# Sliding-window attention with a fused two-layer FFN: ten weight blocks instead of thirteen decoded in the first attention stretch, and two element-wise steps moved between engines

## The chip, the cores and the metric

The kernel runs on one core of one Trainium2 chip. The metric is the device time of one execution in microseconds (us); lower is better. Engines are called PE (TensorE matmuls; PEld are its weight loads), DVE (VectorE), ACT (ScalarE), POOL (GpSimd) and SP (SyncE, which issues the DMAs here).

## What is computed

Four batches of eight heads, 768 positions, head size 64, all fp32. Each query sees the first 4 keys (the sinks) and the last 128 keys up to itself. The heads' outputs are concatenated to rows of 512, and each row goes through an FFN with 2048 hidden values and a clipped quadratic activation.

```python
scores = q @ k.T / sqrt(64)
keep   = (pos_k < 4) | ((pos_q - pos_k >= 0) & (pos_q - pos_k < 128))
a      = softmax(where(keep, scores, -1e9))
x      = concat_heads(a @ v)                  # 3072 x 512
h      = x @ w_in                             # 3072 x 2048
g      = where(h >= 1, h, where(h <= -1, 0, (h + 1) ** 2 / 4))
out    = g @ w_out
```

## The kernel before

**Work units.** Each half of a head's sequence (384 queries, three tiles of 128) is one *unit*; there are 64. Eight heads of one batch and one half are a *chunk* of 384 output rows; there are 8. The first 16 units (`NATIVE`, chunks 0 and 1) compute scores and values in plain fp32 from pair loads (`load2`, `values2`); from unit 16 on, `load` brings keys `k_r` and queries `r` and splits each into a high and a low part (L231 to L235: ACT makes the high part, POOL or DVE subtracts).

**One unit.** `scores` (L249) writes three score tiles to PSUM; a custom DVE instruction (L253) adds the mask and finds the row peak; ACT takes the exponential (L257); POOL adds a small constant to the row sums (L262), DVE inverts them (L263), and the three tiles are scaled by the result at L275 (ACT) or L277 (DVE). The string `NORM = "vaa"` says which engine scales which tile of units 0 to 15: DVE the first, ACT the other two. `transp` (L326, L336) transposes on PE, ACT copies the result out (L329), and `av2` or `av` (L369, L404) multiplies with the values.

**Weights.** The weights lie in memory as 64-bit words. Each of the 32 blocks (16 of w_in, 16 of w_out, 512 KB raw each) is loaded to a buffer `w` and decoded: three DVE integer operations (L157, L158, L159), an ACT cast to the high part (L160) and a DVE subtraction for the low part (L161). Raw and decoded blocks share a pool of 16 buffers (`wpool`), of which the decoded w_out blocks take more and more, so that late raw loads wait until an earlier raw block has been read by its L159.

**FFN.** For each hidden block j of 16, `stage1` runs 12 matmuls (L445) into `h_ps` (two buffers), then ACT (L452, L453), DVE (L454) and ACT (L455) make `g` and its high part `gh`, and L456 subtracts to the low part `gl`. `stage2` for block j comes two blocks later: nine matmuls (L464) with `gh` twice and `gl` once. In the first chunk's FFN (`row0 == 0`) `gl` is made on POOL, in all others on DVE.

**Order of the work.** PE's order is written by hand: `spread` interleaves two lists of steps by their weights. Stretch 1 is chunk 0's attention with the first `WFIRST` = 13 weight blocks; stretch 2 is chunk 1's attention with chunk 0's FFN and the remaining weight blocks; then each chunk's attention runs beside the FFN of the chunk before it. On the other engines a scheduler sets the order when the program is built. Until the end of stretch 2 the loads go out on SP's queue in the order of the program (`fetch`), so a load that waits for a buffer holds back all loads behind it.

```python
prev = wsteps[:WFIRST]                                           # L514, stretch 1
prev = spread(wsteps[WFIRST:], prev, WLEAD)                      # L529, joins stretch 2
eng = NORM[i] if units.index(u) < NATIVE else "v"                # L273
(nc.gpsimd if row0 == GL_POOL else nc.vector).tensor_tensor(gl, g, gh.bitcast(F32), op=ALU.subtract)
```

Of the kernel before, what the change touches and what calls it, by code (L numbers as in the profile page):

```python
# [8 lines left out]
F32 = mybir.dt.float32  # L9
# [4 lines left out]
ALU = mybir.AluOpType  # L14

B, H, S, D = 4, 8, 768, 64
# [11 lines left out]
NATIVE = 16  # L28


KL_POOL = range(16, 20)
GL_POOL = 0
NORM = "vaa"

CHECK = range(34, 34 + 2 * NJ)
WFIRST = 13
AHEAD = 3

LAG = 2
# [9 lines left out]
def attn_ffn(ctx, tc, qk, vx, vs, qp, vp, par, w_in, w_out, out):  # L51
    nc = tc.nc
# [185 lines left out]
    def scores(u, i):  # L238
        b, h, t0 = u
        qs, k_s = st["qk", u]  # L240
        if i == 0:
            st["p", u] = [att.tile([P, CT, 260], F32, name="p"), att.tile([P, 2 * CT], F32, name="stat")]
        p, stat = st["p", u]
        t = t0 + i
        lo = KB if t == 0 else 0
        c0 = i * KB if t0 else max(0, (i - 1) * KB)
        ps = ps_a.tile([P, 512], F32, name="ps_a")
        for j, q in enumerate(qs):
            nc.tensor.matmul(ps[:, lo:260], lhsT=q[:, i * P:(i + 1) * P], rhs=k_s[:, c0:c0 + 260 - lo],  # L249
                             start=(j == 0), stop=(j == len(qs) - 1))  # L250
        peak_i = peak[:, units.index(u), i:i + 1]
        m = (m0, m1n if units.index(u) < NATIVE else m1, m2)[min(t, 2)]
        found = nc.vector.tensor_tensor_reduce(  # L253
            out=p[:, i, lo:260], in0=ps[:, lo:260], in1=m, scale=-0.125, scalar=3.0e38,
            op0=ALU.add, op1=ALU.min, accum_out=peak_i)
        last_max.append(found)
        nc.scalar.activation(p[:, i, lo:260], p[:, i, lo:260], AF.Exp, bias=peak_i, scale=-1.0,  # L257
                             accum_out=stat[:, i:i + 1])
        if i < CT - 1:
            return  # L260
        st.pop(("qk", u))
        nc.gpsimd.tensor_scalar(stat[:, CT:2 * CT], stat[:, 0:CT], 1.0e-9, None, op0=ALU.add)  # L262
        nc.vector.reciprocal(stat[:, CT:2 * CT], stat[:, CT:2 * CT])  # L263
        i0 = int(t0 == 0)
        c0 = 0
        if units.index(u) >= NATIVE:

            c0 = P
            nc.vector.tensor_tensor(p[:, i0:, KB:260], p[:, i0:, KB:260], p[:, i0:, 0:P], op=ALU.add)
        for i in range(CT):  # L270
            lo = KB if t0 + i == 0 else c0
            r = stat[:, CT + i:CT + i + 1]
            eng = NORM[i] if units.index(u) < NATIVE else "v"  # L273
            if eng == "a":
                nc.scalar.activation(p[:, i, lo:260], p[:, i, lo:260], AF.Copy, scale=r)  # L275
            else:
                (nc.gpsimd if eng == "p" else nc.vector).tensor_scalar(p[:, i, lo:260], p[:, i, lo:260], r, None,  # L277
                                                                       op0=ALU.mult)
        if units.index(u) < NATIVE:
            sk = None  # L280
        else:
            sk = att.tile([P, CT * NSINK], F32, name="sk")[:, :(CT - i0) * NSINK]
            nc.vector.tensor_copy(sk.rearrange("p (i s) -> p i s", s=NSINK), p[:, i0:, P:KB])
        st["p", u] = (p, sk)
# [128 lines left out]
    units = [(b, h, t0) for b, t0 in chunks for h in range(H)]  # L413

    def attn_steps(n):
        us = {k: units[n - k] for k in (-1, 0, 1, 2) if 0 <= n - k < len(units)}
        steps = []
        for deep, late, f in ((3, 4, load2), (2, 1, values2)):
            for p in range(NATIVE // 2):
                if n == (2 * p - late if p >= deep else 0):  # L420
                    steps.append((0.0, lambda p=p, f=f: f(*divmod(p, H // 2))))
        if n == 0:
            steps = [steps[i] for i in (0, 3, 1, 4, 2)]
        if n + 1 >= NATIVE and -1 in us:
            steps.append((0.0, lambda: load(us[-1])))
        if 1 in us and n - 1 >= NATIVE:
            steps.append((0.0, lambda: values(us[1])))
        qk = [(0.43 if n < NATIVE else 0.22, lambda i=i: scores(us[0], i)) for i in range(CT) if 0 in us]
        tp = [(0.43, lambda i=i: transp(us[1], i)) for i in range(2 if n - 1 < NATIVE else 1) if 1 in us]
        pv = [(1.0, lambda: av(us[2]))] if 2 in us else []  # L430
        if 2 in us and n - 2 < NATIVE:
            pv = [(1.6, lambda: av2(units[n - 3]))] if n % 2 else []
        steps += qk + tp + pv
        if n in CHECK:
            steps.append((0.0, lambda: recheck(n - CHECK[0], min(n, len(units) - 1))))
        return steps


    def stage1(x, j, ct, hs, row0):
        T = CT * P  # L440
        if ct == 0:
            hs[j] = ps_h.tile([P, 512], F32, name="h_ps")
        h_ps = hs[j]
        for n, (w, y) in enumerate(((0, 0), (0, 1), (1, 0))):
            nc.tensor.matmul(h_ps[:, :T], lhsT=w_i[j][:, w, ct * P:(ct + 1) * P], rhs=x[:, y, ct],  # L445
                             start=(ct == 0 and n == 0), stop=(ct == NCT - 1 and n == 2))
        if ct < NCT - 1:
            return
        g = moe.tile([P, T], F32, name="g")
        gh = moe3.tile([P, T], F32R, name="gh")  # L450
        gl = moe3.tile([P, T], F32R, name="gl")
        nc.scalar.activation(g, h_ps[:, :T], AF.Relu, bias=half, scale=0.5)  # L452
        nc.scalar.activation(g, g, AF.Square)  # L453
        nc.vector.scalar_tensor_tensor(g, g, 1.0, h_ps[:, :T], op0=ALU.min, op1=ALU.max)  # L454
        nc.scalar.copy(gh, g)  # L455
        (nc.gpsimd if row0 == GL_POOL else nc.vector).tensor_tensor(gl, g, gh.bitcast(F32), op=ALU.subtract)  # L456
        hs[j] = gh, gl

    def stage2(o_ps, hs, j, tt, row0):
# [18 lines left out]
    def moe_steps(row0, tail):  # L478


        x = xpool.tile([P, 2, NCT, CT * P], F32R, name="x")
        o_ps, hs = [], {}
        steps = [(0.0, lambda ct=ct: split(x, ct)) for ct in range(NCT)]
        second = tail[:]
        for j in range(NJ):
            if j < LAG:
                steps += second[j * CT:(j + 1) * CT]
            steps += [(0.49, lambda j=j, ct=ct: stage1(x, j, ct, hs, row0)) for ct in range(NCT)]
            if j >= LAG:
                steps += [(0.65, lambda j=j - LAG, tt=tt: stage2(o_ps, hs, j, tt, row0)) for tt in range(CT)]  # L490
        tail[:] = [(0.65, lambda j=j, tt=tt: stage2(o_ps, hs, j, tt, row0)) for j in range(NJ - LAG, NJ)
                   for tt in range(CT)]
        return steps

    def spread(a, b, lead=1.0):

        wa, wb = (sum(w for w, _ in s) for s in (a, b))
        steps, n, da, db = [], 0, 0.0, 0.0
        for step in b:
            while n < len(a) and da * lead * wb <= db * wa:  # L500
                steps.append(a[n])
                da += a[n][0]
                n += 1
            steps.append(step)
            db += step[0]
        return steps + a[n:]
# [6 lines left out]
    first.append(early.enter_context(tc.tile_pool(name="first", bufs=3)))  # L513
    prev = wsteps[:WFIRST]  # L514
    n0 = 0
    tail = []
    for c in range(len(chunks)):
# [10 lines left out]
        if c == 0:  # L528
            prev = spread(wsteps[WFIRST:], prev, WLEAD)  # L529

# [143 lines left out]
```

## Time and profile before

| | |
|---|---|
| time, median of 3 runs | 725.88 us (724.31 to 726.3) |
| profiled execution: its own time, its span | 726.5 us, 724.8 us |
| PE busy, PEld busy | 97%, 85% of the span |
| DVE, ACT, POOL busy | 73%, 70%, 42% |
| mean granted PE clock | 0.992 |
| chain that ended last, by engine | PE 70%, DVE 13%, ACT 6%, DMA 5%, POOL 3% |

The span is the time from the first to the last instruction. The chain that ended last is followed back from the last instruction, at each step to what released it. "Idle before" is time in which an engine stood still, with the instruction or transfer that ended it. Stretch 1 lasts to about 54 us, where the first FFN matmul starts; stretch 2 to about 144 us.

### The profile page before, as it was taken

To read this page: it belongs to the slowest core of one execution; us is meant where nothing else is said; L and a number is where in the kernel's file an instruction comes from. 1 tells how busy PE (TensorE), PEld (TensorE's weight loads), DVE (VectorE), ACT (ScalarE), POOL (GpSimd) and SP (SyncE) were. 2 spreads that over 40 slices of the span, in tenths; PEclk is the share of its full clock that TensorE was granted. 3 is DMA by queue.
4 is the path that set the end of the run, shared out by engine and by line. 5 is a ranking of instruction groups with operands and counts; after the bars stand their busy time and mean duration, and the time that the engine had idled before them with its cause. 6 is when DMAs were issued, how large, how long until landed. Compare 5 with 4: busy or idle time off the path is not lost.

```text
span 724.8 us, 12264 instructions
## 1 busy us (share of the span) xinstructions
PE 699.7 (97%) x3841; PEld 615.6 (85%) x3841; DVE 529.4 (73%) x1393; ACT 504.4 (70%) x1313; POOL 305.7 (42%) x529
## 2 busy tenths in 40 slices
PE   6879999999999999999999999999999999999996
PEld 4547778899989999999889998999989989989895
DVE  8988989578786777687887887878877787833221
ACT  5887677687776777687677877778777867644432
POOL 3002224755453545455564666645556365500000
PEclk9989999999999999999999999999999999999999
DMA  7453453222221322153242533334323342101001
GB/s 291 146 225 127 188 193 121 58 89 58 57 57 33 96 65 66 46 186 114 88 125 64 170 126 115 115 103 137 122 82 127 107 125 74 67 1 44 0 1 48
DMA packets 38568, 73.54 MB, mean 101 GB/s; under 512 B 6752, under 2 KB 21088, under 8 KB 38496
## 3 DMA queue, kind: packets, MB, share of 16 engines
q1 hardware_dynamic: 38496, 72.68, 31.2%
q8 instruction: 32, 0.52, 0.3%
q14 instruction: 40, 0.33, 0.1%
HBM read 66.37 MB, written 6.29 MB: 100 GB/s over the span
## 4 chain that ended last, share of the span: by engine, by line
PE 70%; DVE 13%; ACT 6%; DMA 5%; POOL 3%; issue 2%; POOLq 0%; ACTq 0%; SPq 0%; DVEq 0%
PE h_ps L445 28%; PE o_ps L464 28%; PE ps_a L249 6%; PE ps_a L404 4%; ACT p L257 2%; PE ps_a L336 2%; DVE k_s L233 2%; DMA k_r<-qk 1%; DVE p L277 1%; PE ps_a L369 1%; PE ps_a L326 1%; DMA r<-vx 1%; DVE gl L456 1%; ACT k_s L231 1%; DMA r<-qk 1%
## 5 line engine op out<-in xcount | busy, mean ns | idle before, releaser
L445 PE MATMUL h_ps<-x,wi 128*128 128x384 f32 x1536 | 310.1, 340 | 0.0
L445 PEld LDWEIGHTS h_ps<-x,wi 128*128 128x128 f32 x1536 | 262.7, 188 | 10.8 <-issue 2.7
L464 PE MATMUL o_ps<-w,gh 128*128 128x512 f32 x768 | 243.6, 398 | 0.0
L464 PE MATMUL o_ps<-w,gl 128*128 128x512 f32 x384 | 150.9, 393 | 0.3 <-POOL gl L456 0.3
L464 PEld LDWEIGHTS o_ps<-w,gh 128*128 128x128 f32 x768 | 134.1, 188 | 15.8 <-issue 1.4
L454 DVE SCALAR_TENSOR_TENSOR g<-g,h_ps 128x384 f32<-128x384 f32 x128 | 70.2, 548 | 66.4 <-ACT g L453 65.5
L452 ACT ACTIVATE g<-h_ps,half 128x384 f32<-128x384 f32 x128 | 73.9, 577 | 62.0 <-PE h_ps L445 61.6
L257 ACT ACTIVATE p<-p,peak 128x260 f32<-128x260 f32 (+1 forms) x192 | 94.0, 490 | 30.7 <-DVE peak L253 29.2
L235 POOL TENSOR_TENSOR q_l<-r,q_h 128x384 fp32r<-128x384 f32 x48 | 50.4, 1049 | 131.9 <-ACT q_h L234 121.6
L455 ACT CAST gh<-g 128x384 fp32r<-128x384 f32 x128 | 65.5, 511 | 53.0 <-DVE g L454 52.1
L456 DVE TENSOR_TENSOR gl<-g,gh 128x384 fp32r<-128x384 f32 x112 | 70.2, 627 | 24.7 <-ACT gh L455 23.7
L464 PEld LDWEIGHTS o_ps<-w,gl 128*128 128x128 f32 x384 | 72.0, 188 | 18.2 <-POOL gl L456 0.8
L253 DVE CUSTOM_DVE_ANT_0 p<-ps_a,m 128x260 f32<-128x260 f32 (+1 forms) x176 | 68.2, 398 | 16.6 <-PE ps_a L249 15.9
L233 DVE TENSOR_TENSOR k_s<-k_r,k_s 64x524 fp32r<-64x524 f32 (+1 forms) x44 | 47.2, 1073 | 42.8 <-ACT k_s L231 42.7
L453 ACT ACTIVATE g<-g 128x384 f32<-128x384 f32 x128 | 67.0, 524 | 2.6
L348 POOL TENSOR_SCALAR_AFFINE_SELECT pt<-pt 128x384 fp32r<-128x384 f32 (+1 forms) x96 | 50.3, 525 | 23.8 <-DVE pt L341 21.8
L277 DVE TENSOR_SCALAR p<-p,stat 128x132 f32<-128x132 f32 (+1 forms) x160 | 56.8, 404 | 0.2
L262 POOL TENSOR_SCALAR stat<-stat 128x3 f32<-128x3 f32 x64 | 28.6, 447 | 66.1 <-ACT p L257 61.4
L346 POOL TENSOR_SCALAR_AFFINE_SELECT pt<-pt 128x384 fp32r<-128x384 f32 (+1 forms) x96 | 52.6, 549 | 6.9 <-ACT pt L340 2.7
L404 PEld LDWEIGHTS ps_a<-pt,v_s 128*128 128x128 f32 x304 | 46.5, 188 | 2.2
L404 PE MATMUL ps_a<-pt,v_s 128*128 128x256 f32 (+1 forms) x304 | 46.4, 272 | 0.0
L249 PE MATMUL ps_a<-k_s,q_h 128*128 128x260 f32 (+1 forms) x144 | 40.4, 281 | 4.4 <-DVE sk L343 3.1
(116 smaller groups left out, 986.1 us busy)
## 6 DMA issues: line engine op xcount, KB each, us to landing
r<-qk SPq DMA_DIRECT2D x48, 192.0 KB
k_r<-qk SPq DMA_DIRECT2D x32, 262.0 KB
w<-w_in SPq DMA_DIRECT2D x16, 512.0 KB
w<-w_out SPq DMA_DIRECT2D x16, 512.0 KB
again<-w_in SPq DMA_DIRECT2D x16, 512.0 KB
again<-w_out SPq DMA_DIRECT2D x16, 512.0 KB
out<-o SPq DMA_DIRECT2D x23, 256.0 KB
r<-vx SPq DMA_DIRECT2D x32, 128.0 KB
```

The costliest lines, as they stand in the source:

```text
L249: nc.tensor.matmul(ps[:, lo:260], lhsT=q[:, i * P:(i + 1) * P], rhs=k_s[:, c0:c0 + 260 - lo], start=(j == 0), stop=(j == len(qs) - 1))
L253: found = nc.vector.tensor_tensor_reduce(out=p[:, i, lo:260], in0=ps[:, lo:260], in1=m, scale=-0.125, scalar=3.0e38, op0=ALU.add, op1=ALU. ...
L257: nc.scalar.activation(p[:, i, lo:260], p[:, i, lo:260], AF.Exp, bias=peak_i, scale=-1.0, accum_out=stat[:, i:i + 1])
L277: (nc.gpsimd if eng == "p" else nc.vector).tensor_scalar(p[:, i, lo:260], p[:, i, lo:260], r, None, op0=ALU.mult)
L404: nc.tensor.matmul(z, lhsT=w, rhs=y, start=(n == 0), stop=(n == len(mms) - 1))
L445: nc.tensor.matmul(h_ps[:, :T], lhsT=w_i[j][:, w, ct * P:(ct + 1) * P], rhs=x[:, y, ct], start=(ct == 0 and n == 0), stop=(ct == NCT - 1 a ...
L452: nc.scalar.activation(g, h_ps[:, :T], AF.Relu, bias=half, scale=0.5)
L453: nc.scalar.activation(g, g, AF.Square)
L454: nc.vector.scalar_tensor_tensor(g, g, 1.0, h_ps[:, :T], op0=ALU.min, op1=ALU.max)
L455: nc.scalar.copy(gh, g)
L456: (nc.gpsimd if row0 == GL_POOL else nc.vector).tensor_tensor(gl, g, gh.bitcast(F32), op=ALU.subtract)
L464: nc.tensor.matmul(o_ps[tt], lhsT=gg[:, tt * P:(tt + 1) * P], rhs=w_o[j][:, w], start=(j == 0 and n == 0), stop=(j == NJ - 1 and n == 2))
```

## The change

`WFIRST` falls from 13 to 10: three weight blocks move from stretch 1 to stretch 2. `gl` of the first chunk is made on DVE as in all other chunks. `NORM` gets an entry for each of the first two chunks: units 8 to 15 scale their first tile on ACT instead of DVE.

```diff
-GL_POOL = 0
-NORM = "vaa"
+NORM = ("vaa", "aaa")
 ...
-WFIRST = 13
+WFIRST = 10
 ...
-            eng = NORM[i] if units.index(u) < NATIVE else "v"
+            eng = NORM[units.index(u) // H][i] if units.index(u) < NATIVE else "v"
 ...
-        (nc.gpsimd if row0 == GL_POOL else nc.vector).tensor_tensor(gl, g, gh.bitcast(F32), op=ALU.subtract)
+        nc.vector.tensor_tensor(gl, g, gh.bitcast(F32), op=ALU.subtract)
```

The changed file is one line shorter, so that in its rows below every line number is one less (L158 there is L159 before).

The first place is DVE in stretch 1, units 8 and 9, from the inversion of unit 8's sums to the next unit's first peak. Before:

```order
L263 RECIPROCAL stat<-stat 128x3
L253 ISA p,peak<-ps_a,m_106 128x260
L253 ISA peak 128x1
L157 TENSOR_SCALAR o<-w 128x512
L277 TENSOR_SCALAR p<-p,stat 128x128
L161 TENSOR_TENSOR w<-o,w 128x512
L158 SCALAR_TENSOR_TENSOR o<-w,o 128x512
L263 RECIPROCAL stat<-stat 128x3
L159 SCALAR_TENSOR_TENSOR o<-w,o 128x512
L277 TENSOR_SCALAR p<-p,stat 128x128
L161 TENSOR_TENSOR wi_157<-o,wi_157 128x512
L253 ISA p,peak<-ps_a,m_109 128x128
```

The same stretch of a pair in the changed kernel (units 4 and 5):

```order
L262 RECIPROCAL stat<-stat 128x3
L252 ISA p,peak<-ps_a,m_106 128x260
L252 ISA peak 128x1
L156 TENSOR_SCALAR o<-w 128x512
L276 TENSOR_SCALAR p<-p,stat 128x128
L160 TENSOR_TENSOR wi_154<-o,wi_154 128x512
L157 SCALAR_TENSOR_TENSOR o<-w,o 128x512
L262 RECIPROCAL stat<-stat 128x3
L158 SCALAR_TENSOR_TENSOR o<-w,o 128x512
L276 TENSOR_SCALAR p<-p,stat 128x128
L252 ISA p,peak<-ps_a,m_109 128x128
```

One subtraction fewer stands between the pair's last scaling and the next peak; the rows ahead of that are the same kinds in the same order.

The second place is DVE late in stretch 2, around the decode of the block `wi14` (raw load `w_1155` before, `w_1198` now). `p_1367` before and `p_1363` now are unit 16's scores, `g_1326` is the activation of hidden block 10. Before:

```order
L161 TENSOR_TENSOR w_1249<-o_1250,w_1249 128x512
L159 SCALAR_TENSOR_TENSOR o_1297<-w_1155,o_1297 128x512
L157 TENSOR_SCALAR o_1337<-w_1247 128x512
L158 SCALAR_TENSOR_TENSOR o_1337<-w_1247,o_1337 128x512
L161 TENSOR_TENSOR wi14_165<-o_1297,wi14_165 128x512
L159 SCALAR_TENSOR_TENSOR o_1337<-w_1247,o_1337 128x512
L454 SCALAR_TENSOR_TENSOR g_1326<-g_1326,h_ps_1303 128x384
L161 TENSOR_TENSOR w_1336<-o_1337,w_1336 128x512
L253 ISA p_1367,peak_97<-ps_a_1369,m0_109 128x128
```

With the change:

```order
L453 SCALAR_TENSOR_TENSOR g_1326<-g_1326,h_ps_1297 128x384
L157 SCALAR_TENSOR_TENSOR o_1283<-w_1159,o_1283 128x512
L157 SCALAR_TENSOR_TENSOR o_1314<-w_1198,o_1314 128x512
L252 ISA p_1363,peak_97<-ps_a_1365,m0_109 128x128
L252 ISA peak_97 128x1
L252 ISA p_1363,peak_97<-ps_a_1374,m1_107 128x260
L252 ISA peak_97 128x1
L455 TENSOR_TENSOR gl_1328<-g_1326,gh_1327 128x384
L158 SCALAR_TENSOR_TENSOR o_1283<-w_1159,o_1283 128x512
L252 ISA p_1363,peak_97<-ps_a_1388,m2_106 128x260
L252 ISA peak_97 128x1
L158 SCALAR_TENSOR_TENSOR o_1314<-w_1198,o_1314 128x512
```

The third integer operation of `wi14` (L159 before, L158 now) stood ahead of hidden block 10's `g` and of unit 16's first peak; now it stands behind both and behind unit 16's last peak.

The third place is SP's queue in the changed kernel at the same point. The second row is the load of the w_in block that gets `wi14`'s raw buffer, the third and fourth are unit 17's keys and queries:

```order
L145 DMA w<-w_out 128x1024
L145 DMA w<-w_in 128x1024
L145 DMA k_r<-qk 128x392
L145 DMA r<-qk 128x384
L145 DMA w<-w_out 128x1024
```

Before, the same rows stand in the same order: nothing moved here.

## Rows read from the trace of the kernel before

**Rows 1.** The page's first part: busy time, share of the span and instructions of each engine.

```profile
PE 699.7 (97%) x3841; PEld 615.6 (85%) x3841; DVE 529.4 (73%) x1393; ACT 504.4 (70%) x1313; POOL 305.7 (42%) x529
```

**Rows 2.** Busy time by stretch of time: length, then busy us and instructions of PE, PEld, DVE, ACT and POOL, the granted PE clock, the DMA share and GB/s. The first three are periods of a pair of units in stretch 1, the rest is stretch 2.

```profile
20.80:31.00 10.20, 7.93 (x43) 4.94 (x42) 9.90 (x31) 9.12 (x31) 1.06 (x3) 0.94 0.60 216
31.00:41.20 10.20, 7.89 (x43) 4.96 (x42) 9.90 (x33) 9.01 (x28) 0.82 (x3) 0.83 0.62 220
41.20:51.40 10.20, 7.81 (x41) 4.96 (x40) 9.28 (x30) 8.81 (x27) 0.46 (x2) 0.83 0.61 223
...
54.40:94.00 39.60, 39.60 (x209) 29.88 (x209) 34.24 (x80) 29.26 (x79) 8.62 (x11) 1.00 0.40 144
94.00:119.00 25.00, 25.00 (x132) 19.45 (x131) 23.77 (x49) 17.43 (x45) 8.31 (x8) 1.00 0.54 190
119.00:132.60 13.60, 13.31 (x84) 11.41 (x84) 13.35 (x34) 10.28 (x30) 9.72 (x12) 1.00 0.31 93
```

**Rows 3.** PE in order of time, stretch 1, units 8 and 9 (start, length, operation, count; in brackets the idle time before it and what ended it).

```profile
41.16 2.40 PE L369 MATMUL ps_a<-pt,v_s 128*64 128x128 f32 x12
...
43.75 1.36 PE L249 MATMUL ps_a<-qp 64*128 64x128 f32 x6
...
49.82 0.80 PE L326 MATMUL ps_a<-ident,p 128*128 128x128 f32 x2 [2.05 <-ACT p L275]
...
51.40 2.40 PE L369 MATMUL ps_a<-pt,v_s 128*64 128x128 f32 x12
...
54.00 0.48 PE L249 MATMUL ps_a<-qp 64*128 64x128 f32 x2
```

**Rows 4.** DVE in order of time at the end of the same pair.

```profile
53.34 0.69 DVE L161 TENSOR_TENSOR wi<-o,wi 128x512 fp32r<-128x512 f32 x1 [1.30 <-ACT wi L160]
54.52 0.29 DVE L253 CUSTOM_DVE_ANT_0 p<-ps_a,m 128x128 f32<-128x128 f32 x1 [0.49 <-PE ps_a L249]
```

**Rows 5.** DVE's groups from 10 to 55 us, by shape: count, busy us, mean ns of one, idle before.

```profile
L158 DVE SCALAR_TENSOR_TENSOR o<-w,o 128x512 int32<-128x512 int32 x13 | 8.9, 684 | 0.0
L159 DVE SCALAR_TENSOR_TENSOR o<-w,o 128x512 int32<-128x512 int32 x13 | 8.8, 677 | 0.0
L157 DVE TENSOR_SCALAR o<-w 128x512 int32<-128x512 int32 x14 | 5.9, 419 | 0.0
L161 DVE TENSOR_TENSOR wi<-o,wi 128x512 fp32r<-128x512 f32 x7 | 4.8, 687 | 2.0 <-ACT wi L160 2.0
...
L277 DVE TENSOR_SCALAR p<-p,stat 128x128 f32<-128x128 f32 x10 | 2.8, 280 | 0.1
```

**Rows 6.** The same groups of DVE from 55 to 136 us.

```profile
L158 DVE SCALAR_TENSOR_TENSOR o<-w,o 128x512 int32<-128x512 int32 x19 | 16.8, 884 | 0.2
L159 DVE SCALAR_TENSOR_TENSOR o<-w,o 128x512 int32<-128x512 int32 x19 | 15.2, 801 | 0.0
L157 DVE TENSOR_SCALAR o<-w 128x512 int32<-128x512 int32 x19 | 9.4, 493 | 2.3 <-DMA w<-w_in 2.3
...
L161 DVE TENSOR_TENSOR w<-o,w 128x512 fp32r<-128x512 f32 x10 | 7.9, 788 | 0.2 <-ACT w L160 0.2
```

**Rows 7.** POOL's largest group from 55 to 136 us.

```profile
L456 POOL TENSOR_TENSOR gl<-g,gh 128x384 fp32r<-128x384 f32 x13 | 15.3, 1178 | 31.8 <-ACT gh L455 18.5 <-issue 13.1
```

**Rows 8.** The same operation on DVE after 160 us: shortest, median and longest ns, first and last start.

```profile
L456 DVE TENSOR_TENSOR gl<-g,gh x107: 540/559/1855, 161.3 to 697.3; 128x384 fp32r<-128x384 f32 x107
```

**Rows 9.** ACT's groups from 10 to 55 us, by shape: an operation on a 128x128 tile.

```profile
L257 ACT ACTIVATE p<-p,peak 128x128 f32<-128x128 f32 x8 | 3.2, 397 | 0.9 <-POOL stat L262 0.4 <-DVE stat L263 0.3 <-DVE peak L253 0.2
```

**Rows 10.** DVE in order of time, late in stretch 2 (the first row is the L159 of `wi14`, the second hidden block 10's `g`, the third unit 16's second peak).

```profile
114.00 0.68 DVE L159 SCALAR_TENSOR_TENSOR o<-w,o 128x512 int32<-128x512 int32 x1
...
117.57 0.54 DVE L454 SCALAR_TENSOR_TENSOR g<-g,h_ps 128x384 f32<-128x384 f32 x1
...
119.55 0.42 DVE L253 CUSTOM_DVE_ANT_0 p<-ps_a,m 128x260 f32<-128x260 f32 x1
```

**Rows 11.** SP's issues in order of time at that point.

```profile
114.70 0.33 SPq L146 DMA_DIRECT2D w<-w_in  x1
115.15 0.36 SPq L146 DMA_DIRECT2D k_r<-qk  x1
```

**Rows 12.** The chain that ended last, in order of time: start, us, what.

```profile
115.15 3.68 DMA k_r<-qk
```

**Rows 13.** ACT in order of time: the high part of unit 17's keys.

```profile
118.85 0.52 ACT L231 CAST k_s<-k_r 128x392 fp32r<-128x392 f32 x1 [0.55 <-DMA k_r<-qk]
```

**Rows 14.** POOL in order of time: unit 17's keys, a `gl`, unit 17's queries.

```profile
119.50 1.03 POOL L233 TENSOR_TENSOR k_s<-k_r,k_s 64x392 fp32r<-64x392 f32 x1 [3.60 <-ACT k_s L231]
120.61 1.35 POOL L456 TENSOR_TENSOR gl<-g,gh 128x384 fp32r<-128x384 f32 x1
121.92 1.46 POOL L235 TENSOR_TENSOR q_l<-r,q_h 128x384 fp32r<-128x384 f32 x1
```

**Rows 15.** PE in order of time, stretch 2: unit 16's last score tile, unit 17's first one, and a matmul on `gl` near the end.

```profile
119.72 0.28 PE L249 MATMUL ps_a<-k_s,q_l 128*128 128x260 f32 x1
...
122.92 0.22 PE L249 MATMUL ps_a<-k_s,q_h 128*128 128x128 f32 x1
123.43 0.33 PE L249 MATMUL ps_a<-k_s,q_l 128*128 128x128 f32 x1 [0.29 <-POOL q_l L235]
...
144.75 0.50 PE L464 MATMUL o_ps<-w,gl 128*128 128x512 f32 x1 [0.33 <-POOL gl L456]
```

## The prediction

> **What bounds the kernel now.** I read the page's first part, the stretches of time, PE's timeline in stretch 1, the other engines' groups, and the timelines of all five queues around 120 us. PE is busy 97% of the span [rows 1], so only time in which PE stands still, or runs at its lower clock, can be won or lost. The stretches show two regimes [rows 2]. In stretch 1 a pair of units takes 10.2 us three times over; PE is busy under 8 us of it, and its mean granted clock falls to 0.83, which says that it spends part of each period at the lower of its two levels (1.2 and 2.4 GHz). DVE is busy 9.9 of 10.2 us there and looks like the limit. In stretch 2 PE is busy 39.6 of 39.6, 25.0 of 25.0 and 13.31 of 13.60 us at full clock: PE is the limit, and DVE runs just under it at 86%, 95% and 98%.
>
> **Is stretch 1 really bound by DVE?** The path says no. In the third period PE starts a unit's scores at 43.75, its transposes at 49.82 after 2.05 us of idling for ACT's scaled tile, the value product at 51.40, and the next scores at 54.00 [rows 3]. So 6.07 us lie between scores and transposes, and 4.18 us on PE from there to the next scores. The first part runs through DVE's peaks, three decode steps and the inversion; the second part is PE alone. At the period's end DVE waits: 1.30 us for an ACT cast and 0.49 us for PE's new scores [rows 4]. Its high share is decode work that fills slack.
>
> **The change part by part.**
>
> *Three blocks leave stretch 1.* One block costs DVE 0.42 + 0.68 + 0.68 + 0.69 = 2.47 us [rows 5], three 7.4 us (somewhat less in a full queue, since neighbours overlap). The order of the changed kernel shows which instructions go: one block per pair less, and the missing subtraction stands behind the pair's last scaling, in the second part of the period. Between a unit's peaks and its scaling the rows are of the same kinds as before. So the 6.07 us stay, and the 4.18 us are PE's own. Bounds for the stretch: a gain of 3 x 2.1 = 6.3 us if DVE's throughput were the limit after all, and nothing. I take nothing, because DVE is seen waiting at the end of the period [rows 4].
>
> *Scalings to ACT.* Eight DVE operations of 0.28 us [rows 5] become ACT operations; the nearest ACT row for that shape has 0.40 us [rows 9]. Units 10 to 15 and 9 have their transposes in stretch 2, behind PE work. Unit 8's transposes are the ones that PE waits for at 49.82, and ACT now does one more tile ahead of the two that they need: +0.4 us (bounds 0 and 0.4).
>
> *`gl` to DVE.* POOL's 13 in this window take 15.3 us [rows 7]; on DVE one takes 0.56 us [rows 8], so 13 add 7.3 us to a DVE that is 86 to 98% busy. But in this stretch the same decode steps are slower than in stretch 1: 0.88 against 0.68, 0.80 against 0.68, 0.49 against 0.42, 0.79 against 0.69 us [rows 5, 6], 0.49 us a block, 9.4 us over 19 blocks. POOL was nearly idle in stretch 1 and is mostly at `gl` here, so I give `gl` some 7 of the 9.4. The move then costs DVE about nothing (bounds: +7.3 and -2.1 us). The Trainium skill ("Perfetto Trace Analysis", section on optimizing Scalar/DVE operations) would offload a saturated DVE to ScalarE or even GpSimd, which speaks against this part; but it adds that offloading between DVE and GpSimd might not help, since they share an SBUF port. The Trainium skill's page "SBUF — State Buffer", section "Who interferes with whom", makes that an exclusive lock: a DVE instruction with two SBUF inputs and a GpSimd instruction that reads SBUF hold each other up. By the first rule alone the move costs the full 7.3 us of DVE; the slower decode steps agree with the second.
>
> PE's two short waits for POOL go: 0.29 us before unit 17's queries (counted in the next term) and 0.33 us for a `gl` at 144.75 [rows 15]: -0.3 us.
>
> *Three blocks join stretch 2.* Their 7.4 us of DVE time fit into its gaps and the quiet 10 us behind 133 us. What does not fit is the **order**. The raw load of the second last w_in block takes the buffer of `wi14`'s raw words. It goes out at 114.70, when the L159 that started at 114.00 is through [rows 10, 11]; unit 17's keys stand right behind it in SP's queue, go out at 115.15 [rows 11] and land 3.68 us later [rows 12]. ACT splits them at 118.85 [rows 13], POOL subtracts from 119.50 to 120.53, then does a `gl`, and the queries from 121.92 to 123.38 [rows 14]. PE reaches unit 17's scores at 122.92 and loses 0.29 us [rows 15]. So there are just 2.4 us of slack between the keys' end at 120.53 and 122.92.
>
> In the changed kernel that L159 stands behind hidden block 10's `g`, unit 16's three peaks and a `gl` on DVE. PE's order around units 16 and 17 hardly moves, so those keep their times. From `g` at 117.57 [rows 10] DVE has: `g` itself 0.5, two L158 1.3, three peaks 0.3 + 0.4 + 0.4, `gl` 0.56, two L159 1.3, together 4.8 us less some 0.4 of overlap: 122.0. From the other side, unit 16's last scores are written at 120.0 [rows 15], and a peak and an L159 behind them give 121.1. I take 122.0, because DVE has little idling there. From the old L159's end (114.68) to the keys' end (120.53) it is 5.85 us, and SP, DMA, ACT and POOL steps are unchanged: 127.85. The queries' subtraction, no longer behind a `gl`, takes 1.03 to 1.46 us, so the second matmul runs at about 129.0 instead of 123.43: **+5.5 us** (bounds +4.5 from 121.1, and +7 if the collisions of [rows 6] stretch DVE's steps). PE's queue is in order; the FFN matmuls behind unit 17's scores wait as well. Nothing later gives it back, because PE is the limit from there on.
>
> **Sum:** +0.4 - 0.3 + 5.5 = +5.6 us on the profiled execution's own 726.5 us, 732.1. The median of the runs shown is 0.6 us lower, so I predict **731.5 us**.
>
> **Rivals.**
> - *Stretch 1 pays for it (no change).* If DVE's throughput does set the period of a pair, it falls by up to 2.1 us three times: -6.3, with the late keys -6.3 + 5.6, 725.2 us. For it: 9.9 of 10.2 us busy [rows 2]. Against it: the waits of [rows 4].
> - *Faster.* Stretch 1 gains 3 to 6.3 us and the keys are not late, because DVE, rid of its collisions with `gl`, reaches the deciding L159 before about 117.5 us. Then 719.6 to 722.9 us. Against it: in the changed order unit 16's last peak precedes that L159, and PE writes those scores only at 120.0.
> - *Slower still.* The collisions stay (POOL's own key and query splits) and `gl` costs DVE its full 0.56 us: four more of them ahead of the L159 are +2.2 us, 733.7. It decides if the decode steps in stretch 2 stay at 0.8 to 0.9 us.
> - *The key load is not held.* If the late raw load took another buffer, only -0.3 and +0.4 remain: 726 us. Against it: the load goes out 0.02 us behind that L159's end.
>
> **How the numbers follow.** About 0.3% (2.2 us) is what a measurement of this kernel can tell from no change. Forecast and its worse form 0.66; no change (first and last rival) 0.20; faster 0.14. The forecast's own range is 729 to 735.5. The range of 724.0 to 735.5 takes in the no-change cases and leaves out the faster one and a tail above.
>
> **What would show it.** PE's timeline: an idle of 4 to 6 us before unit 17's first L249, ended by POOL or ACT on `k_s`; unit 17's key load issued at about 122.4 instead of 115.15. The first FFN matmul still at 54 to 55 us, pairs still 10.2 us. Decode steps in stretch 2 back near 0.68 us. Pairs clearly under 10 us would prove the reading of stretch 1 wrong; unit 17's keys in time would prove the main term wrong.

## The result, and the profile after

The changed kernel takes **736.43 us** (median of 4 runs, 735.75 to 737.42) against 726.09 us before: ratio 1.0141, 95% interval 1.0107 to 1.0174. The forecast was 731.5 us in a range of 724.0 to 735.5: the direction was right, the loss nearly twice as large as the sum, and the time 0.9 us above the upper end. Medians and ratios here and below leave disturbed executions out; the one profiled for e7 was such, so that e12 profiles its kernel again.

To see where the time went, each profiled execution is cut at the first matmul of hidden block 0 in the FFN of chunks 0, 1 and 2 (us; the four parts add up to the span; so cut, stretch 2 of the kernel before ends at 146.95). The last column counts the blocks that DVE had decoded at the first cut and 64.6 us later (119.0 in the kernel before).

| kernel | up to the first cut | stretch 2 | next chunk | rest | decoded |
|---|---|---|---|---|---|
| before | 54.41 | 92.54 | 81.52 | 496.31 | 13, 29 |
| before, second profile (e17) | 54.36 | 92.64 | 81.31 | 493.81 | 13, 30 |
| changed | 53.78 | 101.72 | 83.63 | 496.57 | 9, 27 |
| changed, second profile (e15) | 54.84 | 101.56 | 83.73 | 493.74 | 9, 27 |

Stretch 2 and the next chunk repeat to within 0.2 us; the first part differs by 1.1 us and the rest by 3 us between two executions of one kernel (among the kernels of the second table both spread wider). So the loss is **+9.1 us in stretch 2 and +2.3 us in the next chunk**, and nothing outside them is told apart from chance.

The first part of the page, then stretches of time as in [rows 2] (columns as there; from 119 us cut at PE's stall):

```profile
PE 703.0 (96%) x3841; PEld 616.6 (84%) x3841; DVE 526.8 (72%) x1401; ACT 506.7 (69%) x1321; POOL 287.3 (39%) x513
```

```profile
20.80:31.00 10.20, 7.97 (x45) 5.18 (x46) 8.79 (x30) 9.19 (x32) 0.84 (x3) 0.90 0.49 168
31.00:41.20 10.20, 7.89 (x46) 5.04 (x44) 7.50 (x26) 8.28 (x28) 0.45 (x2) 0.83 0.48 169
41.20:51.40 10.20, 7.40 (x42) 4.68 (x40) 7.11 (x23) 8.13 (x28) 0.61 (x2) 0.83 0.45 167
54.40:94.00 39.60, 39.49 (x209) 29.93 (x209) 35.20 (x85) 30.90 (x84) 2.66 (x4) 1.00 0.46 166
94.00:119.00 25.00, 25.00 (x132) 19.32 (x131) 22.01 (x51) 17.43 (x45) 3.45 (x4) 1.00 0.51 181
119.00:122.80 3.80, 3.33 (x21) 2.86 (x20) 3.80 (x12) 2.84 (x11) 0.00 (x0) 1.00 0.00 0
122.80:128.80 6.00, 0.46 (x2) 0.02 (x1) 5.44 (x15) 3.34 (x9) 1.76 (x2) 0.93 0.51 156
128.80:134.60 5.80, 4.96 (x16) 4.39 (x17) 4.10 (x10) 1.91 (x6) 1.19 (x1) 0.50 0.39 116
```

Two things are to be seen. In stretch 1 DVE falls from 9.9 to between 7.1 and 8.8 us of 10.2, and PE does not go faster for it. From 122.8 to 128.8 PE is busy 0.46 of 6.00 us, and in the 5.8 us behind that its granted clock is 0.50, its lower level, so that 4.96 us of work are worth half as much.

PE in order of time in stretch 1, the same pair as [rows 3]:

```profile
40.62 2.27 PE L368 MATMUL ps_a<-pt,v_s 128*64 128x128 f32 x12
...
49.37 0.88 PE L325 MATMUL ps_a<-ident,p 128*128 128x128 f32 x2 [2.23 <-DVE wi L160]
...
51.03 2.19 PE L368 MATMUL ps_a<-pt,v_s 128*64 128x128 f32 x12
```

This period is 10.4 us, against 10.2 before; in the second profile 10.7.

PE in order of time around unit 17's scores, answering to [rows 15]:

```profile
122.86 0.40 PE L463 MATMUL o_ps<-w,gl 128*128 128x512 f32 x1
128.85 0.47 PE L248 MATMUL ps_a<-k_s,q_h 128*128 128x128 f32 x1 [5.59 <-POOL k_s L232]
130.12 0.47 PE L248 MATMUL ps_a<-k_s,q_l 128*128 128x128 f32 x1 [0.79 <-POOL q_l L234]
130.39 1.16 PE L463 MATMUL o_ps<-w,gh 128*128 128x512 f32 x2
...
132.21 1.16 PE L444 MATMUL h_ps<-x,wi 128*128 128x384 f32 x3
```

And what it waits for: SP's issues, then DVE, answering to [rows 11] and [rows 10].

```profile
122.27 0.33 SPq L145 DMA_DIRECT2D w<-w_in  x1
123.09 0.33 SPq L145 DMA_DIRECT2D k_r<-qk  x1
```

```profile
117.92 0.54 DVE L453 SCALAR_TENSOR_TENSOR g<-g,h_ps 128x384 f32<-128x384 f32 x1
118.38 1.28 DVE L157 SCALAR_TENSOR_TENSOR o<-w,o 128x512 int32<-128x512 int32 x2
...
121.56 0.68 DVE L158 SCALAR_TENSOR_TENSOR o<-w,o 128x512 int32<-128x512 int32 x1
122.16 0.68 DVE L160 TENSOR_TENSOR w<-o,w 128x512 fp32r<-128x512 f32 x1
```

The third integer step of `wi14` runs at 121.56 instead of 114.00, the raw load goes out at 122.27, unit 17's keys at 123.09 instead of 115.15, and PE idles 5.59 + 0.79 us instead of 0.29.

DVE's groups from 55 to 136 us by shape, answering to [rows 6] (count, busy us, mean ns, idle before):

```profile
L157 DVE SCALAR_TENSOR_TENSOR o<-w,o 128x512 int32<-128x512 int32 x22 | 15.0, 687 | 0.1
L158 DVE SCALAR_TENSOR_TENSOR o<-w,o 128x512 int32<-128x512 int32 x21 | 14.2, 683 | 0.0
L160 DVE TENSOR_TENSOR w<-o,w 128x512 fp32r<-128x512 f32 x11 | 9.2, 834 | 0.7 <-ACT w L159 0.7
L156 DVE TENSOR_SCALAR o<-w 128x512 int32<-128x512 int32 x21 | 8.7, 423 | 3.8 <-DMA w<-w_in 3.1 <-DMA w<-w_out 0.6
L455 DVE TENSOR_TENSOR gl<-g,gh 128x384 fp32r<-128x384 f32 x12 | 8.0, 663 | 0.5 <-ACT gh L454 0.4
```

The integer steps fell from 0.88 and 0.80 to 0.69 and 0.68 us once `gl` had left POOL; the subtraction of the w_out blocks did not (0.79 to 0.83 us).

The 2.3 us of the next chunk, in PE's order and, ahead of it, ACT's:

```profile
166.91 0.59 ACT L470 COPY o<-o_ps 128x512 f32<-128x512 f32 x1 [2.64 <-DMA out<-o]
```

```profile
169.94 2.35 PE L444 MATMUL h_ps<-x,wi 128*128 128x384 f32 x12 [0.90 <-DVE g L453]
172.95 0.50 PE L463 MATMUL o_ps<-w,gl 128*128 128x512 f32 x1 [0.19 <-DVE gl L455]
...
175.73 0.36 PE L248 MATMUL ps_a<-k_s,q_h 128*128 128x260 f32 x1 [0.33 <-DVE xn L406]
```

ACT waits until the first of chunk 0's three output tiles is written, to use its buffer for the third. Exponentials and a ReLU stand behind that copy. Before, the same wait was 1.0 us and PE never felt it. PE's three waits are 1.4 us together; where the other 0.9 us went, at full clock, no row shows.

### The profile page after: what moved, and what is told of

Read it like the earlier page. It is cut to its first block, busy times and chain, and to the rows that moved or that the text cites. A ratio compares the mean times of both kernels' runs of the same rounds, so it can differ in the third digit from the quotient of the medians.

```text
span 735.7 us, 12243 instructions
## 1 busy us (share of the span) xinstructions
PE 703.0 (96%) x3841; PEld 616.6 (84%) x3841; DVE 526.8 (72%) x1401; ACT 506.7 (69%) x1321; POOL 287.3 (39%) x513
## 4 chain that ended last, share of the span: by engine, by line
PE 68%; DVE 15%; ACT 7%; DMA 4%; issue 3%; POOL 2%; ACTq 0%; SPq 0%; POOLq 0%
PE o_ps L463 27%; PE h_ps L444 27%; PE ps_a L248 6%; PE ps_a L403 3%; ACT p L256 2%; PE ps_a L368 2%; DVE gl L455 2%; DVE k_s L232 2%; PE ps_a L325 1%; PE ps_a L335 1%; DVE p L276 1%; DVE p L252 1%; DVE g L453 1%; DMA again<-w_in 1%; DMA r<-qk 1%
## 5 line engine op out<-in xcount | busy, mean ns | idle before, releaser
L455 DVE TENSOR_TENSOR gl<-g,gh 128x384 fp32r<-128x384 f32 x128 | 80.2, 627 | 27.3 <-ACT gh L454 26.3
L276 DVE TENSOR_SCALAR p<-p,stat 128x132 f32<-128x132 f32 (+1 forms) x152 | 54.9, 414 | 0.1
```

What stands on the lines that cost most here:

```text
L455: nc.vector.tensor_tensor(gl, g, gh.bitcast(F32), op=ALU.subtract)
```

## The experiments

**Theory A** (the prediction's): the loss is unit 17's key load, late because the orders of DVE and SP hold it. **Theory D**: DVE's time is what stretch 2 lacks; whatever is added to DVE there comes out as waiting of PE, at the keys or elsewhere. **Theory K**: PE's lower clock behind the idle is a loss of its own. **Theory O**: the loss in the next chunk is ACT's wait for an output buffer.

The profiled executions, cut as above:

| kernel | time, us | ratio to before | first cut | stretch 2 | next chunk | rest | decoded |
|---|---|---|---|---|---|---|---|
| e1 ten blocks only | 733.9 | 1.0105 [1.0078, 1.0132] | 54.89 | 101.12 | 81.31 | 493.70 | 9, 27 |
| e2 `gl` only | 728.47 | 1.0034 [1.0019, 1.0050] | 54.52 | 92.74 | 83.33 | 497.80 | 13, 29 |
| e3 scalings only | 726.52 | 0.9998 [0.9980, 1.0016] | 55.24 | 92.94 | 81.31 | 495.74 | 13, 29 |
| e4 keys first | 730.87 | 1.0060 [1.0040, 1.0080] | 54.13 | 98.01 | 82.08 | 494.63 | 9, 27 |
| e5 filled | 736.78 | 1.0150 [1.0129, 1.0172] | 55.48 | 99.25 | 81.77 | 498.68 | |
| e6 copy on DVE | 735.7 | 1.0133 [1.0112, 1.0153] | 54.86 | 102.17 | 83.73 | 494.92 | |
| e7, e12 keys, values | 729.6 (e12: 733.4) | 1.0062 [1.0037, 1.0086] | 55.87 | 98.74 | 82.77 | 494.21 | 10, 27 |
| e8 twelve blocks | 730.31 | 1.0059 [1.0042, 1.0077] | 56.80 | 95.49 | 82.89 | 495.02 | 11, 28 |
| e9 more DVE | 732.35 | 1.0081 [1.0066, 1.0096] | 54.51 | 98.42 | 81.35 | 497.69 | 13, 27 |
| e10 less DVE | 729.16 | 1.0036 [1.0024, 1.0049] | 54.88 | 93.85 | 84.17 | 495.63 | 9, 29 |
| e11 output buffer | 735.48 | 1.0123 [1.0103, 1.0143] | 56.65 | 102.11 | 83.01 | 495.60 | |
| e13 earlier decode | 740.08 | 1.0187 [1.0170, 1.0205] | 54.89 | 105.97 | 82.35 | 496.19 | 9, 27 |
| e14 earlier, keys | 734.88 | 1.0120 [1.0100, 1.0141] | 54.70 | 99.73 | 82.44 | 496.78 | 9, 26 |
| e16 filled, second profile | 732.3 (one run) | | 53.83 | 100.82 | 81.35 | 494.58 | |

**The three parts alone, on the kernel before.**

```diff
-WFIRST = 13
+WFIRST = 10                                   # e1
-        (nc.gpsimd if row0 == GL_POOL else nc.vector).tensor_tensor(gl, ...
+        nc.vector.tensor_tensor(gl, ...       # e2
-NORM = "vaa"
+NORM = ("vaa", "aaa")                         # e3
```

> The kernel before with WFIRST = 10 and nothing else. Theory A (order: unit 17's keys wait behind a raw load that waits for the third integer step of wi14, and it took all three decode blocks and the gl steps on DVE to push that step behind unit 16's peaks): the step stands ahead of the peaks here, so it runs between 116 and 119.5, the keys go out 2 to 5 us later than the 115.15 of before instead of 8, PE idles 0 to 3 us before unit 17's scores, and the time is 726 to 730. Rival B (the three extra blocks alone do it): idle of 5 to 6.5 us there and 734 to 737. Rival C (gl on DVE does it alone): 725 to 726.

> The kernel before with chunk 0's gl on DVE and nothing else. Theory A: the step of wi14 stands ahead of unit 16's peaks and the decode steps in stretch 2 fall back towards 0.68 us, so the keys are in time: 725 to 726, the two short waits of PE for POOL gone. Rival C (gl on DVE costs its 0.56 us each and delays the keys by itself): the keys go out 3 us late or more, 730 to 737. Rival B as A.

> The kernel before with units 8 to 15 scaling their first tile on ACT and nothing else. Theory A and rivals B and C: no place of the chain moves but unit 8's transposes, 0 to 0.4 us later: 725.5 to 726.5. A rival of its own (ACT becomes late in stretch 2): over 728.

The three blocks alone cost stretch 2 +8.6 us. That is rival B of e1 in kind, not A, though the 733.9 us lie just under B's 734 and only 3.7 of PE's 6.6 us of idle stand at unit 17's scores. In e1 the step of `wi14` stands ahead of unit 16's peaks, as A wanted, and the keys go out as late as in the changed kernel all the same; PE stalls there, and once more before that:

```profile
122.80 0.33 SPq L146 DMA_DIRECT2D k_r<-qk  x1
```

```profile
122.21 0.44 PE L326 MATMUL ps_a<-ident,p 128*128 128x128 f32 x2 [1.64 <-DVE peak L253]
...
128.41 0.33 PE L249 MATMUL ps_a<-k_s,q_h 128*128 128x128 f32 x1 [2.87 <-POOL k_s L233]
129.54 0.33 PE L249 MATMUL ps_a<-k_s,q_l 128*128 128x128 f32 x1 [0.81 <-POOL q_l L235]
```

`gl` alone costs stretch 2 nothing (+0.2 us) but brings a loss in the next chunk (+1.8 us): ACT's wait is 2.54 us there too, and 1.0 us in e1 and e3. Its 728.47 us lie between A's forecast and C's. The scalings alone cost nothing that the median can tell. The three ratios add up to the change's: 1.05, 0.34 and -0.02% make 1.37%, against 1.41%.

**Keys ahead of the late raw loads (e4).** On the changed kernel:

```diff
-            for k in range(n, min(n + min(AHEAD, NJ - n // 2 - 1) + 1, 2 * NJ)):
+            for k in range(n, min(n + (min(AHEAD, NJ - n // 2 - 1) if n != 29 else 0) + 1, 2 * NJ)):
 ...
             prev = spread(wsteps[WFIRST:], prev, WLEAD)
+            p31 = prev.index(wsteps[31]); prev.insert(p31 + 3, prev.pop(p31))
```

> The changed kernel, but the raw load of the last w_in block is issued by that block's own step, behind unit 17's keys, and the last w_out block's step three places later, behind unit 18's keys; all decode work stays. Theory A: unit 17's keys go out at 115 to 116, the idle of 6.4 us before its scores and the low clock behind it go, 8.5 us less than the changed kernel: 727 to 729, or 725.5 to 727 if the later wait of ACT for an output buffer (2.3 us) goes with it. Rival B (DVE simply has too much to do in stretch 2): PE waits at the same place or a little later for a decoded block or for g, 733 to 737.

The keys go out at 115.25, in time, and 5.6 us of the 10.3 come back, between A's forecast and B's. But DVE now reaches unit 17's first peak 3.0 us behind the start of its first scores (at 124.13 on PE); PE waits for that at its transposes, and its clock falls again:

```profile
127.12 0.29 DVE L252 CUSTOM_DVE_ANT_0 p<-ps_a,m 128x128 f32<-128x128 f32 x1
```

```profile
127.48 0.55 PE L335 MATMUL ps_a<-ident,p 128*128 128x128 f32 x3 [1.43 <-DVE peak L252]
129.32 0.37 PE L336 MATMUL ps_a<-ident,sk 128*8 128x128 f32 x1 [1.30 <-DVE sk L282]
```

```profile
127.00:129.40 2.40, 0.62 (x5) 0.39 (x5) 2.40 (x12) 1.89 (x7) 0.00 (x0) 0.78 0.00 0
129.40:135.40 6.00, 6.00 (x26) 4.33 (x26) 5.52 (x14) 3.56 (x10) 3.86 (x7) 0.52 0.48 158
```

The key load is about half of the loss, and behind it stands a DVE that is late.

**Idle filled (e5, e16).** On the changed kernel, ahead of the matmuls of `scores`, for unit 17's first tile:

```diff
+        for _ in range(24):
+            nc.tensor.matmul(ps[:, :CT * P], lhsT=w_i[0][:, 0, 0:P], rhs=w_i[0][:, 0, 0:CT * P], start=True, stop=True)
```

> The changed kernel with 24 extra matmuls of 128x384 (some 5.6 us, their results overwritten) on PE right before unit 17's first score tile, where PE idles. Theory K (the idle itself is 6 us, and PE's lower clock behind it costs another 2): the granted clock stays 1.0 from 122 to 136, the matmuls behind the scores run at full speed, PE's idle there is under 1.5 us and the first matmul of hidden block 13 comes about 2 us earlier: 734 to 734.8 us. Rival (the matmuls behind the stall are slow for want of weights or keys): clock 1.0 but no gain, 736 to 737.

> The kernel of e5 once more, for a second profile. Its first profile had 99.25 us for the stretch between the two hidden blocks 0 (the changed kernel 101.72) and 81.8 for the next, but its median did not fall. If the gain in the stretch is real, it is 98.5 to 100 again; if the later loss (498.7 us for the rest against 496.6) is the kernel's own, that comes again too; if both are chance, 101 to 102 and 494 to 498.

The extra matmuls took 4.35 us and not 5.6, and leave idle times of 1.35 and 0.95 us in e5, of 1.38 and 0.94 us in e16. Behind nearly the same idle the clock stayed up in one execution and fell in the other; one row of the stretches of each, e5 first:

```profile
132.00:134.00 2.00, 2.00 (x13) 1.87 (x13) 1.62 (x7) 1.07 (x4) 0.00 (x0) 1.00 0.05 16
```

```profile
132.00:134.00 2.00, 2.00 (x10) 1.91 (x9) 1.10 (x4) 1.39 (x6) 0.00 (x1) 0.50 0.63 233
```

Stretch 2 takes 99.25 and 100.82 us: the clock is worth 1.6 us there, at an otherwise equal schedule (unit 17's first matmul starts 75.05 us behind the first cut in both). In the stretch K gets its 2 us where the clock stayed (2.4 against the changed kernel) and 0.8 where it fell. By the median of five runs the rival's forecast came, and why the gain does not reach the median is open: the later loss of e5 did not come again in e16.

**DVE's load changed and nothing moved (e9, e10).** In e9 the kernel before does one integer step of eleven blocks twice; in e10 the changed kernel leaves it out.

```diff
-        nc.vector.scalar_tensor_tensor(w, x, -0x40000000, w, op0=ALU.bitwise_and, op1=ALU.bitwise_or)
+        for _ in range(again):                # e9: 2 for 16 <= n < 27, e10: 0; else 1
+            nc.vector.scalar_tensor_tensor(w, x, -0x40000000, w, op0=ALU.bitwise_and, op1=ALU.bitwise_or)
```

> The kernel before (thirteen blocks, gl on POOL), but in 11 blocks of stretch 2 (blocks 16 to 26) the second integer step is done twice: 11 x 0.69 to 0.88 = 7.6 to 9.7 us more for DVE, the result unchanged, no load and no block moved. Theory D (in stretch 2 DVE has no time to spare, so what is added to it comes out at its end): hidden block 0 to the next chunk's hidden block 0 goes from 92.5 us to 98 to 103, PE waits around unit 17 and runs at the lower clock behind it: 732 to 737. Rival L (the moved blocks are late because their raw loads and buffers are): 726 to 728.5.

> The changed kernel, but in the same 11 blocks the second integer step is left out (so these weights lack their sign bit and top exponent bit): 7.5 us less for DVE, all loads and buffers as in the changed kernel. Theory D: the stretch falls from 101.7 to 92.5 to 95 us, PE's idle of 6.4 us goes, and the time falls by 7 to 9 us, to 727 to 729.5. Rival L: unit 17's keys still wait behind the raw load, 734 to 737.

Both went as D has it. With thirteen blocks and no block or load moved in the order, 7.6 us or more of DVE time lengthen stretch 2 by 5.9 us, in the same place:

```profile
120.13 0.33 SPq L146 DMA_DIRECT2D w<-w_in  x1
120.57 0.36 SPq L146 DMA_DIRECT2D k_r<-qk  x1
```

```profile
126.58 0.48 PE L249 MATMUL ps_a<-k_s,q_h 128*128 128x128 f32 x1 [2.80 <-POOL k_s L233]
127.98 0.47 PE L249 MATMUL ps_a<-k_s,q_l 128*128 128x128 f32 x1 [0.93 <-POOL q_l L235]
```

With ten blocks and 7.5 us less, the stretch falls from 101.7 to 93.9 us, and the time to 729.16.

**One block moved (e8).** The changed kernel with `WFIRST = 12`.

> The changed kernel with WFIRST = 12 instead of 10: one block moved, gl on DVE, scalings on ACT. Theory D (every moved block adds its 2.5 us to DVE's backlog in stretch 2): between e2's 728.5 for none and 736.4 for three, 730 to 732. Theory A (a threshold: the third integer step of wi14 stands ahead of unit 16's peaks here, so the keys are in time): 727.5 to 729.

Stretch 2 is 95.5 us: +2.8 over e2's 92.7 for one block, +9.0 for three. It grows with the blocks, as D has it, though the step of `wi14` stands ahead of unit 16's peaks. The 2.4 us in its first part are a period of 12.0 us at clock 0.50 in the one execution that was profiled.

**Why DVE's gaps do not take the blocks (e7 and e12, e13, e14).** DVE idles 6.6 us between the first cut and 119 us in the kernel before, 7.5 us in the changed one, and yet it ends late. (The 10 us in the expectations counted a wait that began ahead of the cut.)

```diff
-    for deep, late, f in ((3, 4, load2), (2, 1, values2)):
+    for deep, late, f in ((3, 4, load2), (2, -1, values2)):     # e7, e12, on e4
-WLEAD = 0.75
+WLEAD = 0.55                                                    # e13; e14 with the loads of blocks 30 and 31 behind the keys
```

> As e4_keys_first, and the value loads of the first 16 units come two units later in the order of the program, so that the raw loads behind them on SP's queue are not held. Theory D (DVE is behind with its decode work in stretch 2, and 2.6 us of it are waits for raw loads at 76 and 97 us): those waits go, unit 17's first peak comes 2 to 3 us before the 127.12 of e4, PE's idle of 2.7 us behind it and the low clock go: 726 to 728.5. Rival A (the order alone): 730 to 731 as e4. Another rival: the values come late, PE waits at the value product: over 731.

> The kernel of e7 again, for its profile. Its time did not fall below that of e4, so the forecast of theory D in its simple form (waits for raw loads at 76 and 97 us are what makes DVE late) fails. Either the waits are still there (the loads then wait for something other than the value loads), or they are gone and unit 17's first peak is as late as in e4, 126.5 to 127.5: DVE's order or its rate decides then. About 730.

> The changed kernel with WLEAD = 0.55 instead of 0.75: the decode steps of stretch 2 stand earlier in the order of the work, all else as in the changed kernel. Theory G (DVE idles 10 us between 54 and 119 us because its decode steps are spaced along PE's steps by the written order, and the three blocks therefore come out at the end): that idle falls to 6 to 8 us, and the stretch from 101.7 to 96 to 100 us, since two raw loads still stand ahead of unit 17's keys: 731 to 735. Rival W (the idle is DVE waiting for scores and for ACT at whatever step stands next, the written order changes nothing): idle 10 us, stretch 101 to 103, 736 to 738.

> As e13, and the last w_in block's raw load and decode stand behind unit 17's keys, the last w_out block's behind unit 19's. Theory G: the keys of unit 17 go out at 115 to 116, its first peak comes at 124.5 to 126 instead of e4's 127.1, the stretch is 93 to 95 us, and the time 726.5 to 729. Rival W: as e4, stretch 97 to 99, 730 to 732.

All three forecasts of a gain failed: e7's time is e4's, and e13 and e14 took longer than either side had it. DVE's waits from 55 to 119 us (total, times, longest), the largest of e4 and then of e12:

```profile
DVE o L156 <- DMA w<-w_in: 2.6, 2, 1.5
DVE p L252 <- PE ps_a L248: 2.4, 5, 0.7
```

```profile
DVE p L252 <- PE ps_a L248: 6.3, 8, 2.3
DVE g L453 <- ACT g L452: 1.0, 2, 0.6
```

The waits for raw loads went, and the waits for PE's scores took their place: 7.4 us of idle became 7.8, and unit 17's first peak comes 72.5 us behind the first cut, 73.0 in e4. In e13 and e14 the idle is 7.5 and 8.2 us, and 27 and 26 blocks are decoded at 64.6 us, no more than without the earlier order; what did move are raw loads, ahead of unit 16's keys, and PE stalls there (e14; 5.11 us in e13):

```profile
122.60 0.47 PE L248 MATMUL ps_a<-k_s,q_h 128*128 128x128 f32 x1 [3.82 <-POOL k_s L232]
```

So W has the idle right, which hardly moved, but not the times: these edits also made other loads late. In all of these profiles the gaps are DVE waiting, in its order, for a partner, and these edits of the written order and of the loads only changed the partner. Whether another order of DVE's queue alone could use them was not tried.

**The next chunk (e6, e11).**

```diff
-            nc.scalar.copy(o, o_ps[tt])
+            (nc.vector.tensor_copy if (row0, tt) == (0, CT - 1) else nc.scalar.copy)(o, o_ps[tt])         # e6
-                o = moe.tile([P, DM], F32, name="o")
+                o = first[0].tile([P, QK0], F32, name="qp")[:, :DM] if ... else moe.tile([P, DM], F32, name="o")   # e11
```

> The changed kernel with chunk 0's third output copy on DVE instead of ACT. Theory O (ACT's wait of 2.6 us for an output buffer delays the ReLU and exponentials behind it and costs PE 2.3 us at 170 to 176 us): ACT's wait goes, PE's idle there falls from 1.4 to under 0.4 us: 733.8 to 735. Rival (DVE, which now waits, delays g just as much): 736 to 737.

> The changed kernel, but chunk 0's third output copy goes to a buffer of its own (one of the first 16 units' idle pair buffers) instead of the first copy's. Theory O: ACT does not wait 2.6 us there, PE's idle of 1.4 us at 170 to 176 goes, and the stretch from hidden block 0 of chunk 1 to that of chunk 2 falls from 83.6 to 81.3 to 82 us: 734 to 735. Rival (DVE or the loads make the same delay): 736 to 737.

Neither gave the 2 us back. In e6 DVE waits in ACT's place, with its peaks and `g` behind; in e11 nobody waits for the buffer, but ACT waits for the queries whose load stands behind two output transfers on SP's queue:

```profile
168.64 0.69 DVE L470 COPY o<-o_ps 128x512 f32<-128x512 f32 x1 [3.38 <-DMA out<-o]
```

```profile
171.08 0.52 ACT L233 CAST q_h<-r 128x384 fp32r<-128x384 f32 x1 [2.16 <-DMA r<-qk]
```

O is only half right: the wait is there, but taking it away by an edit uncovers the next one. The profiles in which the wait is short without such an edit have a small loss or none, with `gl` on DVE in all of them: a wait of 0.35 us goes with a next chunk of 81.35 us (e16), 1.89 with 82.35 (e13), 2.64 with 83.63 (changed), 3.00 with 84.17 (e10). So `gl` on DVE does not bring the loss by itself; how long the first output takes decides. Why it takes longer than in the kernel before (it held its buffer 2.1 us after its issue, now 4.0 us, in e16 2.2) stays open.

**Second profiles (e15, e17).** These gave the spread of the parts in the first table. All parts came as expected but the rest, which is 0.3 and 0.2 us under its range.

> The changed kernel once more, for a second profile. If the split of its time holds, hidden block 0 of chunk 0 starts at 53.5 to 56.5 us, the stretch from there to hidden block 0 of chunk 1 takes 101 to 103 us, the next to chunk 2 83 to 84 us, and the rest 494 to 498 us.

> The kernel before once more, for a second profile. Its parts should come within what one execution differs from another: start of hidden block 0 at 53.5 to 56.5, then 92.3 to 93 us, 81.3 to 82 us, and 494 to 498 us.

No version here beats the kernel before: PE idles only 0.6 us in its stretch 2, and stretch 1 did not shorten in any of them by more than single executions differ.

## Why the prediction was wrong, step by step

- **Stretch 1 gains nothing: right.** DVE lost a fifth of its work there and the periods stayed at 9.8 to 10.7 us (10.1 to 10.3 before). Its high share was filling, as the waits of [rows 4] said.
- **Scalings, +0.4 us: not told apart in the time.** e3's ratio is 0.9998 [0.998, 1.0016]. In the period where the term would act, from the value product at 41.29 to the next at 51.82 in e3, the one profile has 10.5 us against 10.2 before.
- **`gl` on DVE costs DVE about nothing: right for stretch 2.** e2 adds 0.2 us there, and the integer steps fell to 0.73 and 0.76 us in e2, to 0.69 and 0.68 in the changed kernel. The Trainium skill's page "SBUF — State Buffer", section "Who interferes with whom", has a DVE instruction with two SBUF inputs and a GpSimd instruction that reads SBUF shut each other out, and the trace agrees (rows in the last section). The full 7.3 us of DVE that the prediction's first rule would give did not appear: from the first cut to 119 us DVE is busy 55.9 us in e2 and 58.0 before. The term missed the next chunk, where the move alone costs 1.8 us (e2) through the output transfers.
- **The waits for POOL's `gl`, -0.3 us: right.** PE's wait at 144.75 has no counterpart.
- **The key load, +5.5 us: right in place and nearly in size.** Issue at 123.09 (forecast 122.4), second matmul at 130.12 (129.0), idle 6.38 against 0.29 us: 6.1 us. Alone it would have left the time inside the range.
- **The step that failed** is "Their 7.4 us of DVE time fit into its gaps and the quiet 10 us behind 133 us. What does not fit is the **order**." It took DVE's idle for free time. By [rows 2] the gaps up to 132.6 us are 6.8 us in all, less than 7.4, and 5.4 of them lie before 94. That idle is waiting on others in a queue in order, and the quiet 10 us come after the point where PE needs DVE. e9 and e10 show that DVE time decides with nothing moved in the order; e1 that the loss comes without the order that the prediction blamed; e1 and e8 that each moved block costs stretch 2 some 3 us. The late key load was the form that the lateness took, and with it mended (e4) a later wait takes half of the gain.
- **Two terms were left at nothing**, the next chunk (+2.3 us) and the clock. PE's idle in stretch 2 grew by 6.3 us (0.62 to 6.96), the stretch by 9.1. Most of the other 2.8 us is busy time at the lower clock: 4.96 us of it, worth half, stand in the row of 128.8 to 134.6. [rows 2] showed the same in stretch 1, as 0.83.

So the forecast's +5.6 became +10.3: 6.3 of idle, 2.8 mostly of clock, 2.3 in the next chunk, and some -1 in parts that vary by more than that.

## What to carry to other kernels

Idle time of an in-order engine is not free capacity: before work is moved into a stretch, ask what each of its gaps waits for, and whether the engine has time left before the point where the bound engine needs its result. A new stall of the matmul engine of several microseconds can have a second price, the lower clock behind it; take it from a stretch of the same trace that has both. And where one late transfer is found behind a queue, look at what made its predecessor late: if an engine's load did, freeing the transfer only shows the next wait.

## What was not expected of the hardware

Behind nearly equal idle times of PE (1.35 and 0.95 us, 1.38 and 0.94 us) the granted clock stayed at 1.00 in one execution of e5's kernel and fell to 0.50 in the other, at a cost of 1.6 us. And of the 32 DVE subtractions of two 128x512 tiles in the changed kernel two take 1.5 us, the others 0.66 to 0.69. These two are the ones that began while POOL was subtracting the queries' high part, and each ends 0.55 us behind POOL's instruction:

```profile
115.21 1.51 DVE L160 TENSOR_TENSOR w<-o,w 128x512 fp32r<-128x512 f32 x1
116.64 0.68 DVE L160 TENSOR_TENSOR wi<-o,wi 128x512 fp32r<-128x512 f32 x1
...
129.14 1.48 DVE L160 TENSOR_TENSOR w<-o,w 128x512 fp32r<-128x512 f32 x1
```

```profile
114.95 1.22 POOL L234 TENSOR_TENSOR q_l<-r,q_h 128x384 fp32r<-128x384 f32 x1
...
128.88 1.19 POOL L234 TENSOR_TENSOR q_l<-r,q_h 128x384 fp32r<-128x384 f32 x1
```

In the kernel before, a DVE subtraction that began first (80.27, with POOL's `gl` at 80.43) took 0.68 us, and POOL's 1.39.
